# Loading one batch's q with four tokens per partition, transposing it for 512 tokens at once, and moving scores ahead of own values, in a fused retention and mixture-of-experts kernel

## The chip, the cores and the metric

The kernel runs on one core of one Trainium2 chip. The metric is the device time of one execution in microseconds (us); less is better. "Span" is the time from the first to the last instruction inside an execution, about 1.7 us less than the device time. Every run also reports the mean granted clock of TensorE as a share of full speed. All runs here are of the fast state; runs of one call share one chip and one set of runs of the kernel before. In the profile lines PE is TensorE, PEld its loading of weights, DVE VectorE, ACT ScalarE and POOL GpSimd. In this kernel the matmuls write to tiles in PSUM, everything else lies in SBUF; copying a PSUM tile to SBUF is called its eviction.

## The reference

```python
# q, k, v: (8 batches, 8 heads, 576 tokens, 64), fp32
scores = (1 / sqrt(64)) * q @ k.transpose          # per batch and head
gamma  = 1 - 2.0 ** (-5 - head)
Dmat   = where(i >= j, gamma ** (i - j), 0)        # causal decay
ret    = (scores * Dmat) @ v
x      = ret.transpose(0, 2, 1, 3).reshape(4608, 512)
p      = domain_probs / domain_probs.sum(-1)       # 4 experts
out    = sum_e p[:, e] * (relu(x @ w1[e]) @ w2[e]) # w1 512 x 1024, w2 1024 x 512
```

## The kernel before

The first part makes the retention output x of batch 0, 512 tokens in four "units" (two halves of the sequence by two groups of four heads) plus a "remainder" of 64 tokens. When x of the first 512 tokens is there, the dense expert matmuls start and go on to the end; later batches' retention is threaded into that stream in numbered slots. On TensorE: `pt` is a transpose, `s` the scores of a unit, `o` its values (own, from masked scores `sT`; carried, from the state `sbd`), `kvp` the products of k and v that make the state, `ph` and `po` the up and down matmuls of the experts, `or` the values of the remainder, `w` matmuls on zeros, put in to keep TensorE's clock up (with five more of them than the changed kernel has, 2 of 24 runs had a low mean clock, without them 16 of 24: f1 to f4, below).

```python
ring = ctx.enter_context(tc.tile_pool(name="ring", bufs=4, space=PSUM))   # every PSUM tile comes from here

def load_unit(raw, b, hf, g, eng):               # two tokens per partition: rows of 512 bytes
    for n, src in srcs:                          # k, q, v
        eng.dma_start(out=raw[n],
                      in_=src[b, 4 * g:4 * g + 4, 2 * C * hf:2 * C * hf + 2 * C, :]
                      .rearrange("h (p r) d -> p h (r d)", r=2))
# ... in values_carried: x is written from PSUM by ScalarE, back to natural token order
nat = lambda ap: ap.rearrange("p (a t r) -> p a r t", a=w, r=2)
src = lambda x, y: o[:, x:y, g, 0:C].rearrange("p a (r t) -> p a r t", r=2)
nc.scalar.activation(nat(xt_of(t)[:, p, lo:hi]), src(a, z), Copy)
# ...
load_w1_at = {1: (slice(0, F // 4),), 2: (slice(F // 4, F // 2), slice(F // 2, 3 * F // 4)),
              3: (slice(3 * F // 4, F),)}        # quarters of the first up weights, issued by GpSimd
# ...
for u in range(NU):
    if u + 2 < NU:
        cast_unit(u + 2)
    if u == NU - 1:
        part = UpHalf(0)
        part.matmuls(0)                          # 8 half-width up matmuls under the last mask
    us[u].values_own()
    if u == 2:
        us[3].kv(False, us[2].reads)
    if u + 1 < NU:
        us[u + 1].scores()
    if u == 1:
        us[2].kv(False, us[1].reads)
    us[u].values_carried()
    if u + 2 < NU:
        us[u + 2].trans_pe(1 - u)
    # ...
# ... slots of the dense stream: 19 scores of the remainder, 20 its values
for at, f in ((11, lambda: rem0.cast(nc.vector)), (11, rem0.trans_dma), (19, rem0.scores), (20, rem0.values)):
    add(at, f)
```

## Time and profile before

| | kernel before |
|---|---|
| device time, median of 6 runs of the same chip | 534.43 us (534.05 to 535.33) |
| span of the profiled run, granted clock | 532.9 us, 1.000 |
| start of the dense stream | 21.82 us |
| first values of the remainder (`or`) | 55.28 us |
| first kv products of batch 1 (`kvp`) | 59.85 us |

Four views matter besides those that the prediction shows. First, the stretch from 8 to 12 us in the view by windows (columns: window, length, busy us and number of instructions of PE, PEld, DVE, ACT and POOL, granted clock, DMA share, GB/s):

```profile
8.00:12.00 4.00, 3.34 (x58) 1.98 (x58) 3.68 (x6) 1.83 (x4) 1.46 (x2) 1.00 1.14 290
```

TensorE is busy 3.34 of 4 us and the clock is at 1.00. Second, ScalarE's copies of `o` into x, which close batch 0, in the groups of the first 30 us (columns: line, engine, operation, tiles, shapes, count, then busy us and mean ns, then the idle time before and what ended it): eight of 256 elements, 454 ns each.

```profile
L634 ACT ACTIVATE xt<-o 128x256 bf16<-128x256 f32 x8 | 3.1, 454 | 2.1 <-PE o L618 2.1
```

Third and fourth, the place where batch 1 enters the dense stream, in the timelines of TensorE and VectorE (columns: start, duration, engine, line, operation, tiles, shape, count, and in brackets the idle time before it and what ended it):

```profile
55.28 0.19 PE L333 MATMUL or<-sTr,bfr_v 128*128 128x64 bf16 x1 [0.37 <-DVE sTr L328]
...
59.51 0.42 PE L550 MATMUL s<-qkT 64*64 64x128 bf16 x16
59.85 0.72 PE L564 MATMUL kvp<-bf_v,bf_k 128*128 128x128 bf16 x8
60.51 0.40 PE L527 MATMUL pt<-ident,bf_k 128*128 128x128 bf16 x4
```

```profile
52.87 0.69 DVE L516 TENSOR_TENSOR bf_q<-raw_q,gq 128x512 bf16<-128x512 f32 x1 [0.21 <-DMA raw_q<-in_q_dram]
...
54.81 0.42 DVE L328 TENSOR_TENSOR sTr<-sr,trir 128x256 bf16<-128x256 f32 x1
...
58.85 1.40 DVE L399 SCALAR_TENSOR_TENSOR acc<-po,pm,acc 128x512 f32<-128x512 f32 x2
```

VectorE waits for the q rows of batch 1 (landed at 52.85), casts them, and only then makes `sTr` (ends 55.23) that `or` waits for at 55.28. So the start of `or` is already set by a transfer and by VectorE's queue behind it, 2.43 us after the rows land, not by TensorE's own work.

### The profile page before, as it was taken

Reading aid. Unit: us, or ns where it says so; the run is one execution under the profiler, and the core shown is the slowest. Engines: PE = TensorE matmul, PEld = TensorE weight load, DVE = VectorE, ACT = ScalarE, POOL = GpSimd, SP = SyncE. Lnnn points to the kernel's source line nnn. Section 1 sums busy time; section 2 is a strip of 40 time slices with the busy share of each in tenths; the row PEclk is TensorE's granted clock in tenths of the full one; section 3 lists DMA queues with packets and bytes.
Section 4 is the critical chain, followed back from the end, with each engine's and each line's share of the span. In section 5 each row is a group of like instructions: output and inputs, shape, how many; then the busy total and the mean of one; then the engine's idle time right before and its main releaser. Section 6 shows DMA issues by size and latency. Waiting matters only on the chain.

```text
span 532.9 us, 10183 instructions
## 1 busy us (share of the span) xinstructions
PE 523.0 (98%) x4212; PEld 341.4 (64%) x4251; DVE 363.1 (68%) x458; ACT 82.4 (15%) x167; POOL 151.8 (28%) x196
## 2 busy tenths in 40 slices
PE   7999999999999999999999999999999999999997
PEld 3644544478745885478646865587548844884486
DVE  5443968895577667697578767776765567557763
ACT  4722430012101111020101101110110000000010
POOL 5833404245244434235232604162000000000000
PEclk9999999999999999999999999999999999999999
DMA  9999977876769766737353664453010111110001
GB/s 238 181 214 219 244 192 183 171 159 163 153 164 158 169 141 149 162 77 173 95 136 92 149 134 115 104 129 116 20 41 25 56 39 41 41 41 20 1 22 59
DMA packets 146414, 63.74 MB, mean 120 GB/s; under 512 B 124608, under 2 KB 137168, under 8 KB 146368
## 3 DMA queue, kind: packets, MB, share of 16 engines
q1 hardware_dynamic: 134912, 43.61, 35.4%
q0 software_dynamic: 11312, 19.35, 16.9%
q8 instruction: 33, 0.54, 0.4%
q14 instruction: 13, 0.11, 0.1%
q10 hardware_dynamic: 144, 0.13, 0.1%
HBM read 53.56 MB, written 9.51 MB: 118 GB/s over the span
## 4 chain that ended last, share of the span: by engine, by line
PE 73%; ACT 2%; issue 0%; DVE 0%
PE ph L348 36%; PE pd L464 34%; ACT xt L291 2%; PE o L283 1%; PE o L278 1%; PE py L464 1%; DVE h L354 0%; PE or L333 0%; PE or L335 0%; PE sr L327 0%; DVE ob L492 0%
## 5 line engine op out<-in xcount | busy, mean ns | idle before, releaser
L348 PE MATMUL ph<-xt,w 128*128 128x512 bf16 x1103 | 248.6, 379 | 2.5 <-DVE h L354 0.2
L354 DVE SCALAR_TENSOR_TENSOR h<-ph,pB 128x1024 bf16<-128x1024 f32 x128 | 156.5, 1224 | 58.6 <-PE ph L348 57.8
L348 PEld LDWEIGHTS <-w 128*128 128x128 bf16 x1136 | 110.2, 98 | 128.5
L464 PEld LDWEIGHTS <-h 128*128 128x128 bf16 x1024 | 100.0, 98 | 13.3
L464 PEld LDWEIGHTS <-s 128*128 128x128 bf16 x768 | 75.0, 98 | 8.8
L464 PE MATMUL pd<-wx,h 128*128 128x256 bf16 x512 | 61.1, 273 | 0.2
L464 PE MATMUL pd<-wx,s 128*128 128x256 bf16 x512 | 61.1, 273 | 0.0
L219 POOL DMA_DIRECT2D pB<-pd x28 | 15.8, 564 | 154.7 <-DVE h L354 145.6
L499 POOL TENSOR_TENSOR ob<-v,p 128x256 f32<-128x256 f32 x15 | 11.8, 784 | 114.7 <-DVE v L496 86.6
L238 POOL TENSOR_TENSOR bf_k<-raw_k,gk 128x512 bf16<-128x512 f32 x24 | 26.1, 1088 | 36.0 <-DMA raw_k<-in_k_dram 16.3
L270 DVE TENSOR_TENSOR sT<-s,tri 128x1024 bf16<-128x1024 f32 x24 | 28.2, 1219 | 6.3 <-PE s L268 6.3
L437 DVE TENSOR_TENSOR s<-s,h 128x1024 bf16<-128x1024 bf16 x32 | 31.5, 1025 | 0.0
L291 ACT ACTIVATE xt<-o 128x768 bf16<-128x768 f32 (+6 forms) x24 | 13.0, 596 | 116.8 <-PE o L283 116.8
L464 PE MATMUL pd<-t4w,h 128*128 128x256 bf16 x256 | 30.6, 273 | 0.0
L387 PE MATMUL po<-wx,h 128*128 128x512 bf16 x123 | 28.7, 379 | 0.4 <-issue 0.2
L464 PE MATMUL pd<-t2w,s 128*128 128x256 bf16 x240 | 28.7, 273 | 0.0
L464 PE MATMUL pd<-t3w,h 128*128 128x256 bf16 x240 | 28.6, 273 | 0.0
L238 POOL TENSOR_TENSOR bf_q<-raw_q,gq 128x512 bf16<-128x512 f32 x24 | 27.0, 1125 | 4.2 <-DMA rawr_v<-in_v_dram 2.2
L472 ACT ACTIVATE p<-pd 128x256 f32<-128x256 f32 x16 | 6.2, 385 | 138.4 <-PE pd L464 106.2
L435 DVE TENSOR_TENSOR s<-h 128x1024 bf16<-128x1024 bf16 x32 | 24.3, 800 | 0.0
L441 DVE TENSOR_TENSOR s<-h,s 128x1024 bf16<-128x1024 bf16 x32 | 24.3, 800 | 0.0
L481 DVE TENSOR_TENSOR u<-pd,p 128x256 f32<-128x256 f32 x15 | 6.4, 425 | 22.3 <-PE pd L464 22.3
(155 smaller groups left out, 376.0 us busy)
## 6 DMA issues: line engine op xcount, KB each, us to landing
pB<-pd POOLq DMA_DIRECT2D x28, 256.0 KB, 3.6
raw_k<-in_k_dram SPq DMA_DIRECT2D x48, 128.0 KB, 2.9
raw_q<-in_q_dram SPq DMA_DIRECT2D x48, 128.0 KB, 3.0
raw_v<-in_v_dram SPq DMA_DIRECT2D x48, 128.0 KB, 3.1
out_dram<-oa SPq DMA_DIRECT2D x16, 256.0 KB, 2.2
out_dram<-ob SPq DMA_DIRECT2D x15, 256.0 KB, 2.2
w<-in_moe_w_dram POOLq DMA_DIRECT2D x3, 1024.0 KB, 13.5
wx<-in_moe_w_dram POOLq DMA_DIRECT2D x3, 1024.0 KB, 14.7
```

Source lines behind the costliest of these rows:

```text
L219: eng.dma_start(out=pB[t, e], in_=pd[e:e + 1, t * NT:(t + 1) * NT].to_broadcast([128, NT]))
L238: eng.tensor_tensor(bfs[p % 2][n], raw1[n], g[:, :, 2 * p:2 * p + 2].unsqueeze(3).to_broadcast([128, NC, 2, D]), op=MULT)
L270: nc.vector.tensor_tensor(sT[:, :, :, :].rearrange("p j c t -> p (j c) t"), s[:, :, :, :].rearrange("p j c t -> p (j c) t"), tri[:, :].uns ...
L291: nc.scalar.activation(xt_of(t)[:, self.ps, n0 + a - t * NT:n0 + z - t * NT], o[:, :, a:z], Copy)
L348: nc.tensor.matmul(ph[:, f, :], lhsT=w1_sb[e][:, dc, fc * 128:(fc + 1) * 128], rhs=x[:, dc, :], start=(dc == 0), stop=(dc == NDC - 1))
L354: nc.vector.scalar_tensor_tensor(h[:, fk:fk + 2, :], ph, 0.0, pB[t, e][:, :].unsqueeze(1).to_broadcast([128, 2, NT]), op0=MAX, op1=MULT)
L387: nc.tensor.matmul(po[:, gg, :], lhsT=h[:, e * NFC + fc, (2 * m + gg) * 128:(2 * m + gg + 1) * 128], rhs=wx[e // 2][:, (e % 2) * NFC + fc, ...
L435: nc.vector.tensor_tensor(self.alloc("s1")[:, l], h[:, l, self.b], h[:, r, self.b], op=ADD)
L437: nc.vector.tensor_tensor(self.alloc("s2")[:, l], self.s1[:, l], h[:, l, self.a], op=SUB)
L441: nc.vector.tensor_tensor(self.alloc("s4")[:, l], h[:, r, self.a], self.s2[:, l], op=SUB)
L464: mm = nc.tensor.matmul(dst, lhsT=src[:, kk, tok], rhs=rhs(c), start=(start and c == 0), stop=(c == KH - 1), skip_group_check=True)
L499: nc.gpsimd.tensor_tensor(self.ob[:, HF:Dm], self.v, self.p5, op=ADD)
```

## The change

The intent: read q of batch 0 in longer rows (four tokens, 1,024 bytes), transpose it for the whole sequence at once, and give VectorE the scores of the next unit before TensorE does the own values of the present one. With it come a different split of the weight loads, another place for the up matmuls, and one slot for the remainder.

```diff
+                nc.sync.dma_start(out=flat(raw0q[u][:, 2 * gg:2 * gg + 2, :, :]),
+                                  in_=q[0, 4 * u + 2 * gg:4 * u + 2 * gg + 2, 0:SM, :]
+                                  .rearrange("h (p r) d -> p h (r d)", r=4))
 ...
-                    nat = lambda ap: ap.rearrange("p (a t r) -> p a r t", a=w, r=2)
-                    src = lambda x, y: o[:, x:y, g, 0:C].rearrange("p a (r t) -> p a r t", r=2)
+                    rr = 2 if self.b else 4
+                    nat = lambda ap: ap.rearrange("p (a t r) -> p a r t", a=w, r=rr)
+                    src = lambda x, y: o[:, x:y, g, 0:C].rearrange("p a (r t) -> p a r t", r=rr)
 ...
+    load_w1_at = {1: quarter[0:1], 2: quarter[1:2], 3: quarter[2:4]}
 ...
     for u in range(NU):
         if u + 2 < NU:
             cast_unit(u + 2)
-        if u == NU - 1:
-            part = UpHalf(0)
-            part.matmuls(0)
-        us[u].values_own()
-        if u == 2:
-            us[3].kv(False, us[2].reads)
         if u + 1 < NU:
             us[u + 1].scores()
-        if u == 1:
-            us[2].kv(False, us[1].reads)
+        if u + 2 < NU:
+            us[u + 2].trans_pe()
+        if u == 3:
+            warm(2)
+        us[u].values_own()
+        if u in (1, 2):
+            us[u + 1].kv(False, us[u].reads)
         us[u].values_carried()
 ...
-    part.matmuls(1)
+    part = [UpHalf(i) for i in range(2)]
+    for i in range(2):
+        part[0].matmuls(i)
+        part[1].matmuls(i)
 ...
-    ... (19, rem0.scores), (20, rem0.values)):
+    ... (19, rem0.scores), (21, rem0.values)):
```

Cut are the tables for four tokens, the casts and transposes of q by themselves, the number of matmuls on zeros (19 before, 16 after), the move of two state copies from VectorE to ScalarE, and the relus of the two up halves, which now both follow the 32 up matmuls.

More of the change, by code (lines that the diff above doesn't have):

```diff
@@ L112 @@
     NU = 4
-    raw0 = [{n: epool.tile([128, 4, 2, D], FP32, name=f"raw0_{u}{n}") for n, _ in srcs} for u in range(NU)]
-    bf0 = {n: spool.tile([128, 2, 2, 2, 4, D], BF16, tag="S", name=f"bf0_{n}") for n, _ in srcs}
+    raw0 = [{n: epool.tile([128, 4, 2, D], FP32, name=f"raw0_{u}{n}") for n in "kv"} for u in range(NU)]
+    raw0q = [epool.tile([128, 4, 4, D], FP32, name=f"raw0_q{g}") for g in range(2)]
+    bf0 = {n: spool.tile([128, 2, 2, 2, 4, D], BF16, tag="S", name=f"bf0_{n}") for n in "kv"}
+    bf0q = spool.tile([128, 2, 4, 4, D], BF16, tag="S", name="bf0_q")
+    q4 = [epool.tile([128, 2, 4, C], BF16, name=f"q4_{g}") for g in range(2)]
     def load_unit(raw, b, hf, g, eng):
         for n, src in srcs:
-            eng.dma_start(out=raw[n],
-                          in_=src[b, 4 * g:4 * g + 4, 2 * C * hf:2 * C * hf + 2 * C, :]
-                          .rearrange("h (p r) d -> p h (r d)", r=2))
+            if n in raw:
+                eng.dma_start(out=raw[n],
+                              in_=src[b, 4 * g:4 * g + 4, 2 * C * hf:2 * C * hf + 2 * C, :]
+                              .rearrange("h (p r) d -> p h (r d)", r=2))
     units0 = ((0, 0), (0, 1), (1, 0), (1, 1))
@@ L125 @@
     for u, (hf, g) in enumerate(units0):
-        load_unit({n: raw0[u][n][:, :, :, :].rearrange("p h r d -> p h (r d)") for n in "kqv"}, 0, hf, g, nc.sync)
+        flat = lambda t: t.rearrange("p h r d -> p h (r d)")
+        load_unit({"k": flat(raw0[u]["k"][:, :, :, :])}, 0, hf, g, nc.sync)
+        if u < 2:
+            for gg in range(2):
+                nc.sync.dma_start(out=flat(raw0q[u][:, 2 * gg:2 * gg + 2, :, :]),
+                                  in_=q[0, 4 * u + 2 * gg:4 * u + 2 * gg + 2, 0:SM, :]
+                                  .rearrange("h (p r) d -> p h (r d)", r=4))
+        load_unit({"v": flat(raw0[u]["v"][:, :, :, :])}, 0, hf, g, nc.sync)
     zz = epool.tile([128, 512], BF16)
@@ L143, with pair_mask @@
     make_identity(nc, ident)
-    tri0 = tpool.tile([128, 2, 2, C // 2], BF16, tag="uv", name="tri0")
-    nc.gpsimd.memset(tri0, 1.0)
-    for a in range(2):
-        nc.gpsimd.affine_select(out=tri0[64 * a:64 * a + 64], in_=tri0[64 * a:64 * a + 64],
-                                compare_op=mybir.AluOpType.is_ge, fill=0.0,
-                                base=0, channel_multiplier=-2, pattern=[[-1, 2], [1, 2], [2, C // 2]])
+    pos_4 = epool.tile([128, 4], FP32)
+    nc.gpsimd.iota(pos_4, pattern=[[1, 4]], base=0, channel_multiplier=4, allow_small_or_imprecise_dtypes=True)
+    def pair_mask(t, r):
+        nc.gpsimd.memset(t, 1.0)
+        for a in range(2):
+            nc.gpsimd.affine_select(out=t[64 * a:64 * a + 64], in_=t[64 * a:64 * a + 64],
+                                    compare_op=mybir.AluOpType.is_ge, fill=0.0,
+                                    base=0, channel_multiplier=-2, pattern=[[-1, 2], [1, r], [r, C // r]])
+    tri4 = epool.tile([128, 2, 4, C // 4], BF16, name="tri4")
+    pair_mask(tri4, 4)
+    tri0 = tpool.tile([128, 2, 2, C // 2], BF16, tag="uv", name="tri0")
     nc.gpsimd.memset(sbd, 0.0)
@@ L160 @@
     decays(gk0, gq0, (lambda o, h: o[:, :, h, :], pos_0))
+    gq4 = const.tile([128, H, 4], FP32, name="gq4")
+    for hh in range(H):
+        nc.vector.tensor_scalar_mul(gq4[:, hh, :], pos_4, -lg[hh])
+    nc.scalar.activation(gq4, gq4, Exp, scale=-1.0, bias=lsc)
     tri = const.tile([128, C], BF16)
@@ L171, in later_tables @@
     def later_tables():
+        pair_mask(tri0, 2)
         nc.gpsimd.memset(tri, 1.0)
@@ L517, in cast, with trans_pe @@
                                  .unsqueeze(3).to_broadcast([128, 4, 2, D]), op=MULT)
-        def trans_pe(self, between=0):
+        def trans_pe(self):
             self.qk = atp.tile([128, 2, 2, 2, C], BF16, tag="qkT", name="qkT0")
             pt = ring_tile("pt", [128, 2, 2, 2, 2 * C], BF16)
-            for i, n in ((1, "k"), (0, "q")):
-                if i == 0 and between:
-                    warm(between)
+            ns = ((1, "k"), (0, "q")) if self.b else ((1, "k"),)
+            for i, n in ns:
                 for r in range(2):
@@ L528, in trans_pe @@
                                             self.bf(n)[:, r, 2 * g:2 * g + 2].rearrange("p j d -> p (j d)"), ident)
-            nc.scalar.activation(self.qk[:, :, :, :, :].rearrange("p i r g t -> p i (r g) t"),
-                                 pt[:, :, :, :, 0:C].rearrange("p i r g t -> p i (r g) t"), Copy)
+            lo = 2 - len(ns)
+            nc.scalar.activation(self.qk[:, lo:2].rearrange("p i r g t -> p i (r g) t"),
+                                 pt[:, lo:2, :, :, 0:C].rearrange("p i r g t -> p i (r g) t"), Copy)
         def trans_dma(self):
@@ L538, in qT @@
         def qT(self, rows, g, a):
+            if self.b == 0:
+                i = 64 * self.hf + 32 * a
+                return q4[self.g][rows, g, :, i:i + 32]
             return self.qk[rows, 0, :, g, 64 * a:64 * a + 64]
@@ L554, in scores @@
                 s[:, :, :, :, :].rearrange("p j g r t -> p (j g) (r t)"),
-                tri0[:, :, :, :].rearrange("p r s t -> p (r s t)").unsqueeze(1).to_broadcast([128, 4, 2 * C]), op=MULT)
+                (tri0 if self.b else tri4)[:, :, :, :].rearrange("p r s t -> p (r s t)").unsqueeze(1).to_broadcast([128, 4, 2 * C]), op=MULT)
         def kv_mm(self, rows, dst, hh, start=False, others=()):
@@ L592, in kv @@
                 else:
-                    self.reads.append(nc.vector.tensor_copy(dst, src) if not fresh and self.g == 0 else nc.scalar.activation(dst, src, Copy))
+                    self.reads.append(nc.scalar.activation(dst, src, Copy))
                 if hf == 0 and self.carry is not None:
@@ L641, in values_carried, with cast_q, trans_q @@
                     a = z
-    bfv0 = lambda g: {(n, hf): bf0[n][:, hf, g] for n in "kqv" for hf in range(2)}
+    bfv0 = lambda g: {(n, hf): bf0[n][:, hf, g] for n in "kv" for hf in range(2)}
     us = [Unit(0, hf, g, raw0[u], bfv0(g)) for u, (hf, g) in enumerate(units0)]
-    warm(8)
-    us[0].cast("k", nc.vector)
-    us[0].cast("q", nc.vector)
-    us[0].cast("v", nc.gpsimd)
-    us[0].trans_pe()
-    warm(3)
-    load_w1_at = {1: (slice(0, F // 4),), 2: (slice(F // 4, F // 2), slice(F // 2, 3 * F // 4)),
-                  3: (slice(3 * F // 4, F),)}
+    def cast_q(g):
+        for gg in range(2):
+            hs = slice(2 * gg, 2 * gg + 2)
+            nc.vector.tensor_tensor(
+                bf0q[:, g, :, hs, :].rearrange("p r h d -> p h r d"), raw0q[g][:, hs, :, :],
+                gq4[:, 4 * g + 2 * gg:4 * g + 2 * gg + 2, :].unsqueeze(3).to_broadcast([128, 2, 4, D]), op=MULT)
+    def trans_q(g):
+        pt = ring_tile("ptq", [128, 2, 4, C], BF16)
+        for gg in range(2):
+            for r in range(4):
+                nc.tensor.transpose(pt[:, gg, r, :], bf0q[:, g, r, 2 * gg:2 * gg + 2, :].rearrange("p j d -> p (j d)"),
+                                    ident)
+        nc.scalar.activation(q4[g], pt, Copy)
+    quarter = [slice(i * F // 4, (i + 1) * F // 4) for i in range(4)]
+    load_w1_at = {1: quarter[0:1], 2: quarter[1:2], 3: quarter[2:4]}
     def cast_unit(u):
         us[u].cast("k", nc.vector)
-        us[u].cast("q", nc.vector)
+        if u < 2:
+            cast_q(u)
         us[u].cast("v", nc.gpsimd)
@@ L658, in cast_unit @@
             load_w1(0, f)
+    warm(8)
+    cast_unit(0)
+    us[0].trans_pe()
+    warm(2)
+    trans_q(0)
+    warm(4)
     cast_unit(1)
+    us[1].trans_pe()
     us[0].scores()
-    warm(4)
-    us[1].trans_pe(2)
+    trans_q(1)
     us[0].kv()
-    warm(1)
     for u in range(NU):
@@ L668 @@
             cast_unit(u + 2)
-        if u == NU - 1:
-            part = UpHalf(0)
-            part.matmuls(0)
-        us[u].values_own()
-        if u == 2:
-            us[3].kv(False, us[2].reads)
         if u + 1 < NU:
             us[u + 1].scores()
-        if u == 1:
-            us[2].kv(False, us[1].reads)
+        if u + 2 < NU:
+            us[u + 2].trans_pe()
+        if u == 3:
+            warm(2)
+        us[u].values_own()
+        if u in (1, 2):
+            us[u + 1].kv(False, us[u].reads)
         us[u].values_carried()
-        if u + 2 < NU:
-            us[u + 2].trans_pe(1 - u)
         if u == 0:
@@ L692 @@
     h = hp.tile([128, E * NFC, NT], BF16, name="h")
-    part.relu(h)
-    part = UpHalf(1)
-    part.matmuls(0)
-    part.matmuls(1)
-    part.relu(h)
+    part[0].relu(h)
+    part[1].relu(h)
     first = ctx.enter_context(ExitStack())
@@ L745 @@
     rem0 = Rem(0)
-    for at, f in ((11, lambda: rem0.cast(nc.vector)), (11, rem0.trans_dma), (19, rem0.scores), (20, rem0.values)):
+    for at, f in ((11, lambda: rem0.cast(nc.vector)), (11, rem0.trans_dma), (19, rem0.scores), (21, rem0.values)):
         add(at, f)
```

## The prediction

> **What bounds the kernel now.** I read the page's busy shares first, then the chain that ended last, then the waits of TensorE, then the timeline of the first 25 us, because the diff touches only batch 0 and one slot later on.
>
> ```profile
> PE 523.0 (98%) x4212; PEld 341.4 (64%) x4251; DVE 363.1 (68%) x458; ACT 82.4 (15%) x167; POOL 151.8 (28%) x196
> PE 73%; ACT 2%; issue 0%; DVE 0%
> ...
> PE s L550 <- ACT qkT L529: 0.5, 1, 0.5
> PE pt L527 <- DVE bf_k L516: 0.4, 1, 0.4
> PE or L333 <- DVE sTr L328: 0.4, 1, 0.4
> ```
>
> TensorE is busy for 523 of 532.9 us and carries the chain; its named waits are a few tenths each. The busy share flatters the start, though: warm-up matmuls on zeros (`w`) count as work, and so does pipeline time. What matters is when the dense stream of 512-column matmuls begins, since after it the order and number of matmuls are the same in both kernels, apart from one slot. In the timeline:
>
> ```profile
> 16.87 0.42 PE L550 MATMUL s<-qkT 64*64 64x128 bf16 x16
> 17.34 1.23 DVE L552 TENSOR_TENSOR sT<-s,tri 128x1024 bf16<-128x1024 f32 x1 [0.88 <-PE s L550]
> 17.45 1.04 PE L369 MATMUL ph<-xt,w 128*128 128x256 bf16 x8
> 18.62 0.42 PE L608 MATMUL o<-sT,bf_v 64*64 64x128 bf16 x16
> 18.97 0.40 PE L618 MATMUL o<-qkT,sbd 128*128 128x128 bf16 x4
> 19.20 2.78 PE L369 MATMUL ph<-xt,w 128*128 128x256 bf16 x24
> ```
>
> This is the end of batch 0. While VectorE masks the last unit's scores (17.34 to 18.57), TensorE does 8 of the 32 half-width up matmuls; own values, carried values and the other 24 follow. 24 matmuls at 0.109 us (8 took 0.87 us from first start to ninth) put the start of the dense stream at 19.20 + 2.62 = **21.82 us**.
>
> What feeds the start is the queue of loads. Each line gives KB and the time from issue to landing:
>
> ```profile
> raw_0k<-in_k_dram SPq DMA_DIRECT2D x1, 256.0 KB, 2.8
> raw_0q<-in_q_dram SPq DMA_DIRECT2D x1, 256.0 KB, 3.1
> raw_0v<-in_v_dram SPq DMA_DIRECT2D x1, 256.0 KB, 4.9
> raw_1k<-in_k_dram SPq DMA_DIRECT2D x1, 256.0 KB, 5.3
> raw_1q<-in_q_dram SPq DMA_DIRECT2D x1, 256.0 KB, 5.6
> ```
>
> With their issue times in the timeline (0.81, 1.33, 1.87, 2.41, 2.96) they land at 3.6, 4.5, 6.8, 7.7 and 8.6: one 256 KB load per 0.90 us (about 290 GB/s), with one stall of 1.4 us before the third.
>
> [...] zero matmuls go from 0.427 to 0.216 us apart at 5.5 us [...] with a granted clock of 1.00.
>
> **The change part by part.**
>
> *Loads.* The same 3 MB in 12 loads, but q of both halves of the sequence comes with the first two units. Order before: k q v, four times. After: k0 q q v0, k1 q q v1, k2 v2, k3 v3. The piece that completes unit 1's q moves from fifth to seventh place. Landings, with the stall in third place as now: k0 3.6, q 4.4, q 6.65, v0 7.55, k1 8.45, q 9.25, **q 10.05**, v1 10.95, k2 11.85, v2 12.7, k3 13.6, v3 14.4. The last comes 0.3 us earlier (4 x 0.10), the first two units 1.5 to 2.2 us later.
>
> *Work.* Transposes of q: 16 before and after. Casts of q: 4 at 0.69 before and after. Copies of transposed data on ScalarE: 4 x 1.025 before; after, 4 of half size at an estimated 0.59 (between the rows of 256 elements at 0.38 to 0.45 and 1,024 at 1.025) and 2 x 1.025, so 4.4 against 4.1 us. Two copies of carried state (2 x 0.42 us) go from VectorE to ScalarE. Zero matmuls: 19 before, 16 after. VectorE gets 8 small multiplies of some 0.1 us before the first load lands, which is free. Nothing large is removed: this is a change of order.
>
> *The path after.* Following the new order of instructions with these durations and about 0.05 us for each handover:
> 1. q lands at 10.05; VectorE casts it: 10.1 to 10.8.
> 2. Four transposes, drained: 11.25. ScalarE copies (1.02): 12.3.
> 3. Scores of unit 1 (0.42): 12.35 to 12.9. Mask (1.22): to 14.2.
> 4. VectorE, in order, casts k of unit 3 only now, though it landed at 13.6: 14.1 to 14.8; transposes from 15.05, copied (0.59) by 16.1.
> 5. TensorE meanwhile: own values of unit 1 (0.25), kv of unit 2 (0.65 with its two switches), carried values (0.11), front of kv for unit 3 (0.44), with switches of tile shape at about 0.09: scores of unit 3 start at 17.0.
> 6. Mask of unit 3: 17.5 to 18.7. Under it lie own values of unit 2, kv of unit 3, carried values of unit 2 and the two new zero matmuls, to 18.85.
> 7. Own and carried values of unit 3: 18.95 to 19.5.
> 8. Then all 32 half-width matmuls, 32 x 0.109 = 3.5: the dense stream starts at **23.0**.
>
> The same reckoning on the order of before gives 22.05 where the trace has 21.82, so I use differences: 23.0 - 22.05 = **+0.95 us**. Of that, 0.87 is step 8: the 8 up matmuls that filled the wait for the last mask now stand behind it, with zero matmuls in their old place. Putting scores ahead of own values does shorten each unit, but the later q of unit 1 eats it.
>
> *Remainder.* Values of the first remainder move one slot (8 matmuls of 0.216 = 1.7 us) later, behind which their wait of **0.37** (listed above) vanishes.
>
> Sum: 534.35 + 0.95 - 0.37 = 534.9 us.
>
> **The rivals.**
> - *The stall before the third load does not come back.* Nothing in the profile says what makes it, and fewer, longer rows may avoid it. Then q of unit 1 lands at 9.0, and the same steps start the dense stream at 21.97, or 0.08 less than before: 534.35 - 0.08 - 0.37 = 533.9 us. I give this one in three.
> - *The weights become the bound.* The second half of the first w2 is issued at 16.75 and lands at 26.8; its first matmul is at 25.27 + 8 x 0.216 = 27.0, a slack of 0.2. Had the change made TensorE earlier by 1 us, the weights would have taken most of it back. With TensorE later, and the load queue relieved by 0.3 us, they do not bind. The same slack caps any gain.
> - *ScalarE becomes the bound of batch 0.* It gets the q copies and both state copies, and the two final copies of o (0.77 a pair) now come in one run of four after the last state copy. The up matmuls of the second half need them at 20.4, they end at about 20.5, and only their fourth quarter is needed last. Close, 0 to 0.3 us.
> - *The clock falls back.* Idle stretches of some 1.3 us (waiting for the second q piece) and 0.7 us are larger than before's[...]. Chance 5%, cost 1 to 2 us.
>
> **Range and chances.** Two thirds of 534.9 and one third of 533.9 give 534.6. The runs of before spread over 1.3 us and the load times are uncertain by about 0.5 us, so 533.5 to 535.7 should hold 8 times in 10. Two per cent is 10.7 us, and the whole of batch 0 takes 22: within 2% is as good as certain.
>
> **What would show it.** In the profile of the changed kernel: the second q piece of unit 1 lands near 10 (9 if the stall is gone); the last carried values at about 19.3 and then 32 half-width matmuls in one run of 3.5 us; the first 512-column matmul near 22.8; no wait of `or` on `sTr`; loads of w2 landing by 27 with no wait on them. The prediction is wrong if q in 1,024-byte rows lands much faster than 0.8 us a piece, if TensorE waits for weights, or if the zero matmuls run at 0.427 us again after 6 us.

The 0.80 us for a 256 KB piece of q in 1,024-byte rows was the author's assumption: the kernel before has no such rows, and its 256 KB loads land 0.90 us apart but for one stall. The 5% for the clock rests on the assumption that idle stretches of 1.3 and 0.7 us leave it alone, which was not shown either. The small terms of the path are in the trace of the kernel before: from the end of a cast on VectorE to the first transpose 0.06 us (5.18 to 5.24), a switch of tile shape 0.10 us (16 matmuls of own values take 0.25 us up to the next start at 10.78, where the same shape follows, and 0.35 at 18.62, where another does), seven small multiplies on VectorE 0.71 us (1.20 to 1.91).

## The result, and the profile after

The changed kernel took **538.37 us** (median of 6 runs, 536.19 to 540.25) against 534.43. A ratio is the mean time of one kernel's fast runs over the mean of the other's of the same rounds, so not quite the ratio of the medians: 1.0072, with a 95% interval of 1.0043 to 1.0102. So it is within 2%, as predicted, but 2.7 us above the top of the range. The spread tripled, too: 4.1 us between runs, against 1.3, and four of the six runs had a mean clock of 0.990 to 0.997. The profile fell on a run of 540.11 us (span 538.4, clock 0.997).

The end of batch 0, in TensorE's timeline, then in ScalarE's groups of the first 30 us, then in ScalarE's timeline:

```profile
19.14 0.40 PE L645 MATMUL o<-q,sbd 128*128 128x128 bf16 x4
19.37 1.67 PE L393 MATMUL ph<-xt,w 128*128 128x256 bf16 x11
21.34 2.45 PE L393 MATMUL ph<-xt,w 128*128 128x256 bf16 x21 [0.30 <-ACT xt L662]
23.84 1.46 PE L372 MATMUL ph<-xt,w 128*128 128x512 bf16 x6
```

```profile
L662 ACT ACTIVATE xt<-o 128x256 bf16<-128x256 f32 x8 | 5.1, 799 | 0.0
```

```profile
18.84 2.45 ACT L662 ACTIVATE xt<-o 128x256 bf16<-128x256 f32 x4
```

The last carried values start at 19.14, where the prediction had 19.3. But the 32 half-width matmuls (11 and 21) are held up twice by the run of four copies on ScalarE, which took 2.45 us; each copy took 799 ns where the kernel before had 454. The last half-width matmul starts at 23.52, so the dense stream begins at 23.63 (the record of its first matmul is missing, the one shown is the second). That is 1.81 us later than before; 0.95 was predicted.

Batch 1's entry, in the timelines of TensorE and VectorE:

```profile
58.28 0.19 PE L357 MATMUL or<-sTr,bfr_v 128*128 128x64 bf16 x1
...
60.78 0.42 PE L577 MATMUL s<-qkT 64*64 64x128 bf16 x16
63.35 0.72 PE L591 MATMUL kvp<-bf_v,bf_k 128*128 128x128 bf16 x8 [2.15 <-DVE acc L423]
...
65.11 2.92 PE L411 MATMUL po<-wx,h 128*128 128x512 bf16 x7 [0.22 <-issue]
```

```profile
55.45 0.69 DVE L540 TENSOR_TENSOR bf_q<-raw_q,gq 128x512 bf16<-128x512 f32 x1 [0.21 <-DMA raw_q<-in_q_dram]
...
57.39 0.42 DVE L352 TENSOR_TENSOR sTr<-sr,trir 128x256 bf16<-128x256 f32 x1
...
61.90 1.40 DVE L423 SCALAR_TENSOR_TENSOR acc<-po,pm,acc 128x512 f32<-128x512 f32 x2
```

The wait of `or` is gone, as predicted. In its place the kv products stand still for 2.15 us until VectorE has done `acc`, the eviction of a `po` tile, at 63.29. They need its PSUM buffer: with one slot later, the ring of four buffers hands the kv products another buffer than before, and in the program's semaphores they wait for `acc` where they had waited for a transpose on TensorE. VectorE is late because the q rows landed at 55.43 instead of 52.85. After the standstill seven `po` matmuls start 0.427 us apart instead of 0.216 (2.92 us for 7): the clock has fallen, to 0.50 from 64.21 to 67.62.

The whole difference of the two profiled spans, 5.5 us, adds up from these lines: dense stream 23.63 - 21.82 = +1.81; the wait of `or` that is gone, -0.54 (in the kernel before, `s` of batch 1 comes 37.69 us after the dense start; after, 37.15); the wait of the kv products, +2.22 (63.35 instead of 60.78 + 0.35); slow clock until own values, +1.68 (4.61 us from kv products to own values at 67.96 instead of 2.93); everything later, +0.33.

### The profile page after: what moved, and what is told of

Read it like the earlier page. It is cut to its first block, busy times and chain, and to the rows that moved or that the text cites. A ratio compares the mean times of both kernels' runs of the same rounds, so it can differ in the third digit from the quotient of the medians.

```text
span 538.4 us, 10193 instructions
## 1 busy us (share of the span) xinstructions
PE 525.3 (98%) x4209; PEld 342.2 (64%) x4248; DVE 363.9 (68%) x464; ACT 85.4 (16%) x172; POOL 153.3 (28%) x200
## 4 chain that ended last, share of the span: by engine, by line
PE 72%; ACT 2%; issue 0%; DVE 0%
PE ph L372 36%; PE pd L488 33%; ACT xt L315 2%; PE o L307 1%; PE o L302 1%; PE py L488 1%; DVE h L378 0%; PE or L357 0%; PE sr L351 0%; PE or L359 0%; DVE ob L516 0%
## 5 line engine op out<-in xcount | busy, mean ns | idle before, releaser
L488 PEld LDWEIGHTS <-h 128*128 128x128 bf16 x1024 | 100.0, 98 | 13.3
L411 PEld LDWEIGHTS <-h 128*128 128x128 bf16 x128 | 12.5, 101 | 15.0 <-issue 1.6
```

The costliest lines, as they stand in the source:

```text
L411: nc.tensor.matmul(po[:, gg, :], lhsT=h[:, e * NFC + fc, (2 * m + gg) * 128:(2 * m + gg + 1) * 128], rhs=wx[e // 2][:, (e % 2) * NFC + fc, ...
L488: mm = nc.tensor.matmul(dst, lhsT=src[:, kk, tok], rhs=rhs(c), start=(start and c == 0), stop=(c == KH - 1), skip_group_check=True)
```

## The experiments

Eighteen further kernels ran, all correct. In the table, "low clock" counts runs with a mean clock of 0.998 or less.

| run | what it is | median us (range) | ratio to before, 95% | low clock |
|---|---|---|---|---|
| changed kernel | | 538.37 (536.19 to 540.25) | 1.0072, 1.0043 to 1.0102 | 4 of 6 |
| e1 | slot 20 back | 537.62 (536.18 to 538.02) | 1.0055, 1.0040 to 1.0070 | 4 of 6 |
| e2 | eviction turned | 537.17 (536.00 to 540.25) | 1.0061, 1.0035 to 1.0087 | 4 of 6 |
| e3 | e1 and e2 | 536.88 (535.36 to 538.09) | 1.0040, 1.0023 to 1.0057 | 4 of 6 |
| e4 | before with slot 21 | 534.28 (533.90 to 535.25) | 0.9999, 0.9986 to 1.0012 | 0 of 6 |
| f1 | changed, 5 zero matmuls more | 537.03 (536.49 to 540.82) | 1.0062, 1.0035 to 1.0088 | 1 of 6 |
| f2 | e3, 5 zero matmuls more | 536.86 (535.36 to 537.67) | 1.0042, 1.0024 to 1.0059 | 1 of 6 |
| f3 | f2, early up matmuls | 536.14 (535.09 to 537.30) | 1.0031, 1.0014 to 1.0048 | 0 of 6 |
| f4 | f2, old order | 536.56 (535.46 to 537.70) | 1.0039, 1.0021 to 1.0056 | 0 of 6 |
| g1 | f3, weights' quarter back | 535.57 (534.98 to 536.48) | 1.0015, 1.0001 to 1.0028 | 0 of 5 |
| g2 | changed, quarter back | 537.59 (535.91 to 538.61) | 1.0049, 1.0030 to 1.0068 | 3 of 6 |
| g3 | before, quarter late | 535.40 (534.76 to 536.70) | 1.0010, 0.9995 to 1.0026 | 0 of 6 |
| g4 | g1, slot 21 | 536.18 (534.98 to 537.19) | 1.0024, 1.0008 to 1.0040 | 2 of 6 |
| h1 | changed, VectorE's order | 539.32 (535.91 to 541.48) | 1.0078, 1.0046 to 1.0110 | 4 of 6 |
| h2 | g1, VectorE's order | 535.38 (534.49 to 536.15) | 1.0015, 0.9999 to 1.0031 | 1 of 6 |
| h3 | before, VectorE's order | 534.09 (533.70 to 536.51) | 1.0001, 0.9981 to 1.0021 | 0 of 6 |
| h4 | f1, slot 20, VectorE's order | 536.84 (536.61 to 538.15) | 1.0046, 1.0031 to 1.0061 | 1 of 6 |
| i1 | f1, the wait lengthened | 538.98 (538.42 to 540.01) | 1.0090, 1.0072 to 1.0107 | 1 of 4 |
| i2 | i1, slot 20 | 540.01 (538.70 to 540.55) | 1.0099, 1.0082 to 1.0117 | 3 of 4 |

In the 51 runs of the kernel before beside these, the mean clock was never under 0.999.

### The slot and the eviction, each alone and together (e1, e2, e3), and the slot in the kernel before (e4)

```diff
 e1, e3:  -(21, rem0.values)
          +(20, rem0.values)
 e2, e3:  -nat = lambda ap: ap.rearrange("p (a t r) -> p a r t", a=w, r=rr)
          +nat = lambda ap: ap.rearrange("p (a t r) -> p a r t" if self.b else "p (a t r) -> p a t r", a=w, r=rr)
          -src = ... .rearrange("p a (r t) -> p a r t", r=rr)
          +src = ... .rearrange("p a (r t) -> p a r t" if self.b else "p a (r t) -> p a t r", r=rr)
 e4:      kernel before, -(20, rem0.values)  +(21, rem0.values)
```

> The changed kernel with one part undone: the values of a unit's remainder stand in the earlier slot again (20 instead of 21). Theory A (buffer rotation): in the changed kernel the first kv products of batch 1 take the buffer that the eviction of po on VectorE frees late (a wait of 2.15 us at 63.35, after which the matmuls ran at 0.43 us instead of 0.21 for about 2.5 us). With the slot back, that wait and the slow matmuls vanish, and a wait of about 0.4 us before those values comes back: about 536.0 us, 2.3 under the changed kernel. Theory B (late transfers): the batch 1 rows land 2.5 us later whatever the slot is, and TensorE waits elsewhere for the same lateness: 537.5 to 538.5 us. Either way the run's first part (dense stream from about 23.6) is as in the changed kernel.

> The changed kernel with the eviction of o to xt on ScalarE turned round in batch 0: it writes neighbouring tokens (2-byte step) and reads PSUM with the step instead; the result stays right. Theory A (the step of the writes costs): an eviction of 128x256 takes 0.35 to 0.45 us instead of 0.80, the last ones end about 0.7 to 1.0 us earlier, the first 512-column matmul stands at about 22.7 instead of 23.6, and the time falls by about 0.9 us if the later wait on the kv products stays as it is (537.4). Theory B (any strided 128x256 eviction costs this): 0.75 to 0.85 us each, no change, 538.3.

> Both edits of the two runs before: values of the remainder back in the earlier slot, and the eviction of batch 0 writing neighbouring tokens. If both theories A hold and add up: 535.1 us, within 0.5 of the kernel before. If neither: 538.3.

> The kernel before with only the values of the remainder moved one slot later (21 instead of 20). Theory A (rotation): the same new dependency of the kv products on the eviction of po, but rows land 2.5 us earlier here and VectorE's eviction ended at 60.25 when the products were due at about 59.85: a wait of 0.4 us in place of the 0.37 us that is taken away: 534.1 to 535.0 us. If the wait is long enough for the clock to fall, 536 to 537. Rival (the slot is a plain gain of 0.37): 534.0.

**The eviction** is settled in the profile; the time of e2 (537.17, 537.4 expected) lies too near that of the changed kernel to show 0.9 us. Turned round, it writes neighbouring tokens and takes its step in PSUM instead; the copies fall from 799 to 381 ns, in ScalarE's groups of the first 30 us of e2:

```profile
L662 ACT ACTIVATE xt<-o 128x256 bf16<-128x256 f32 x8 | 2.6, 381 | 0.3 <-PE o L645 0.2
```

So it is the 8-byte step of the writes that costs, not the four tokens as such: the kernel before writes with a step of 4 bytes at 454 ns.

**The slot** did what theory A said in the profile: with slot 20 (e1, e3) the kv products follow the scores after 0.35 us, with slot 21 (e2) after 1.07, and there they start 0.06 us after `acc` ends, as in the changed kernel. But the times missed: 536.0 was expected of e1 and 537.62 came, which lies in the range of theory B, though no wait stands at batch 1 in e1's profile; of e3 535.1 was expected and 536.88 came. Alone in the kernel before (e4) the slot changes nothing (ratio 0.9999): the wait of `or` went, and the kv products waited 0.05 us more.

Why e1 missed shows in the view by windows of its own profile:

```profile
8.00:12.00 4.00, 2.55 (x51) 1.72 (x52) 3.69 (x5) 2.31 (x5) 1.45 (x2) 0.98 1.20 301
12.00:15.50 3.50, 3.50 (x49) 2.19 (x39) 1.82 (x2) 2.63 (x6) 3.00 (x5) 0.53 1.05 158
```

The granted clock is 0.53 from 12 to 15.5 us, the same in e2 (0.54) and e3 (0.60). The profile of the changed kernel has the same thin stretch, without the fall:

```profile
8.00:12.00 4.00, 2.54 (x42) 1.50 (x41) 3.66 (x5) 2.32 (x4) 1.41 (x2) 1.00 1.21 300
```

In both, TensorE is busy 2.54 to 2.55 of the 4 us from 8 to 12, instead of 3.34 (3.73 in e4), because the new order waits there for the pieces of q, for their casts and for ScalarE's copy, and has fewer matmuls on zeros to fill those waits. This was a new theory (C): too thin a stretch lets the clock fall, in some runs and not in others.

### Holding the clock, and the other parts of the start (f1 to f4)

```diff
 f1 to f4:  -    warm(4)                       +    warm(6)
            +            if self.b == 0 and (self.hf, self.g) == units0[1]:      # in scores()
            +                for _ in range(3):                                     # zeros, overwritten after
            +                    nc.tensor.matmul(s[:, 0].rearrange("p g r t -> p (g r t)"),
            +                                     lhsT=zz[:, 0:128], rhs=zz, start=True, stop=True)
 f2, f3, f4: and the edits of e3
 f3:        -            warm(2)
            +            part = [UpHalf(0)]
            +            part[0].matmuls(0)
 f4:        the loop's order of the kernel before: own values, kv, scores, carried values, transposes
```

> The changed kernel plus five matmuls on zeros in its two emptiest places in batch 0: two more before the k transposes of unit 1, three before its scores (written to the scores' own buffer and overwritten). Three earlier profiles of variants showed the granted clock at 0.5 for 3 to 3.5 us from 12 on, after a stretch of 8.3 to 11.7 in which matmuls streamed only about 0.38 of the time (0.56 or more in the kernel before). Theory C (too thin a stretch lowers the clock at the start in most runs): no matmul at half speed between 6 and 20, mean clock 1.0 in every run that hasn't the long wait at 61 to 63; runs of 537 to 538 become 536.0 to 536.4, the runs at 539 to 540 (wait of the kv products) stay possible. Theory D (the fall is random or from elsewhere): runs at 0.996 to 0.997 as often as in the changed kernel, median 537 to 538.

> The same five zero matmuls, with the values of the remainder back in the earlier slot and the eviction writing neighbouring tokens. Theory C with both theories A: the slow runs vanish altogether, every run has clock 0.999 to 1.0, median 535.4 (that of the two runs of the pair without zeros whose clock was 1.0), spread about 1 us. Theory D: median 536.9 as without the zeros.

> As the run before, and eight half-width up matmuls instead of two matmuls on zeros under the last mask, where the kernel before has them. Prediction's step 8: 8 x 0.109 = 0.87 us leave the end of batch 0, the two zero matmuls (0.43) beside the mask lengthen nothing: 0.5 to 0.9 us less, 534.5 to 534.9. Rival (the up matmuls wait for the eviction of o or for weights there): 535.4, and a wait of the first of them.

> As the second run of this call, with the old order within a unit: own values first, then the scores of the next unit, transposes last. It measures what the order alone is worth, given the new q. If the scores ahead of own values shorten each unit, as the prediction held without a figure: 0.3 to 1.0 us slower than with the new order (535.7 to 536.4). If VectorE's masks and casts decide the pace of the units whatever TensorE's order is: the same within 0.2 us (535.4).

The clock held: none of the four profiles shows a fall after 6.5 us, and 2 of 24 runs had a low mean clock, against 16 of 24 of the changed kernel, e1, e2 and e3. Over everything that ran (without i1 and i2), 23 of 36 runs with the change's zero matmuls have a low clock and 6 of 47 with five more. The 23 average 538.55 us, the other 13 of the 36 average 536.29, so a run with a low clock is 2.3 us longer on average. That the thin stretch lets the clock fall is supported by this; what it should bring to the median is not, as follows.

The traces, cut up afterwards, say which stretches let it fall. In the eight falls of the kept profiles before 520 us the clock stays low for 3.41 us, and each fall comes a whole number of such stretches after the clock's first rise (in the changed kernel's profile it rises at 6.18 and falls at 64.21, 17 of them later). Take the columns of the matmuls that start in each of these stretches, at 0.216 us for 512, and weigh them by the size of their tile as a part of 128*128, the largest in the traces (a quarter for 64*64). In all 20 profiles the eight stretches that end in a fall are filled to between 0.21 and 0.38, and every other one at full clock to 0.41 or more. The plain busy share does not part them: 0.32 to 0.65 before a fall, and down to 0.55 without one. The thinnest stretch in the start of the changed kernel's profile has 0.41, those of e1 to e3 have 0.36 to 0.38: the start lies just at the edge, so where the cuts fall would decide from run to run. This was found after the fact; no run was made to test it.

The pieces of the start can be read from the profiles as the time from the landing of the last q piece to the dense stream:

| run | q complete | dense stream | between | what differs |
|---|---|---|---|---|
| changed | 9.63 | 23.63 | 14.0 | |
| f1 | 9.69 | 23.81 | 14.1 | zeros |
| f2 | 9.64 | 22.84 | 13.2 | and the eviction turned: -0.9 |
| g1 | 9.57 | 22.35 | 12.8 | and up matmuls early: -0.4 |
| f4 | 10.09 | 24.19 | 14.1 | f2 with the old order: +0.9 |
| e3 | 9.63 | 24.11 | 14.5 | f2 without zeros, clock fell: +1.3 |
| e1 | 9.41 | 24.81 | 15.4 | f1 without zeros, clock fell: +1.3 |

f2 in TensorE's timeline has all 32 half-width matmuls in one run and the dense stream at 22.84:

```profile
19.35 3.66 PE L393 MATMUL ph<-xt,w 128*128 128x256 bf16 x32
22.84 2.32 PE L372 MATMUL ph<-xt,w 128*128 128x512 bf16 x10
...
56.59 0.19 PE L357 MATMUL or<-sTr,bfr_v 128*128 128x64 bf16 x1 [0.66 <-DVE sTr L352]
```

But the medians hardly moved (f1 537.03 where 536.2 was expected, f2 536.86 where 535.4 was). The last of these lines shows where the gain went: `or` now waits 0.66 us for `sTr`, which ended 2.38 us after the q rows of batch 1 landed at 54.16. In each of the four profiles with slot 20 that have this wait and VectorE's old order (before, f2, g1, g3) the values of the remainder start 2.43 us after those rows; in each of the five with slot 21 in which the kv products wait for `acc` (changed, e2, e4, f1, g4) these start 7.5 to 7.9 us after them. An earlier start of the dense stream is given back there when the rows are late. In f1 TensorE also loses 0.56 us at 174 us to a transfer of remainder rows, which the profile of the kernel before does not show.

f3 landed at 536.14, 1.2 us over its expected range. Its eight early up matmuls do run under the last mask, but 0.58 us of the gain was lost because the second half's matmuls stood ahead of the first half's rest and waited for ScalarE; g1 mends that. f4 lost 0.9 us at the start by the old order, so **scores ahead of own values gain 0.9 us at the start**. That is one profile each, but the measure repeats well: f1, h4, i1 and i2, whose starts are equal, have 14.12 to 14.13 us. The median of f4 (536.56) is not above f2's: the gain at the start does not show in the time.

### Why the rows are late (g1 to g4)

```diff
 g1, g2, g4:  -load_w1_at = {1: quarter[0:1], 2: quarter[1:2], 3: quarter[2:4]}
              +load_w1_at = {1: quarter[0:1], 2: quarter[1:3], 3: quarter[3:4]}
 g3:          kernel before, the third quarter moved from unit 2 to unit 3
 g1, g4:      built on f3, the first half's up matmuls finished first; g4 with (21, rem0.values)
```

> The kernel with five zero matmuls, turned eviction, earlier slot and early up matmuls, and now also the third quarter of the first up weights issued with unit 2, as the kernel before has it, and the first half's up matmuls finished before the second half's begin. Theory E (the quarter that the change issues 1.3 us later leaves the software queue idle, and everything behind it in that queue, up to the rows of batch 1, lands about 1.2 us later, where VectorE's casts and then TensorE wait for them): w2 of the third expert pair lands at 51 to 51.5 instead of 51.5 to 53.8, the q rows of batch 1 at 52.9 or so, dense stream from about 22.2, time 534.2 to 534.8, spread 1.5 us. Rival (the lateness comes from elsewhere, from chip to chip or run to run): landings as in the profile without this edit (53.2), 535.5 to 536.2.

> The changed kernel with that quarter alone issued with unit 2 again. Theory E: rows of batch 1 land 1.2 us earlier, the wait of the kv products at 61 to 63 shrinks to under 1 us in nearly every run, so no runs at 539 to 540.8, while the start stays as it was: 536 to 537.8, median 537.0. Rival: runs at 539 and more as often as in the changed kernel (3 of 6).

> The kernel before with that quarter alone issued with unit 3, as the change does. Theory E: the software queue idles about 1.2 us, rows of batch 1 land about 1.2 us later, and the wait of the remainder's values, 0.37 us, grows by as much: 535.4 to 535.8 us. Rival (the queue catches up, or the rows weren't what that wait came from): 534.3 to 534.7.

> The first kernel of this call with the values of the remainder in the change's slot. With the rows on time, the wait of about 0.4 us for the remainder goes and the wait of the kv products stays under 0.3: 533.9 to 534.5, the best of all, level with the kernel before or up to 0.5 better. If the rows are late in some runs, those show 536 to 538.

Theory E is not confirmed as the main cause. Only g3 came as it expected (535.40); g1 (535.57) lies in the rival's range, g2 (537.59, 537.0 expected) had three runs of 538.5 to 538.6, and g4 (536.18) took 1.7 us more than expected. With the quarter late, the q rows of batch 1 landed at 55.43 (changed kernel) and at 53.16 to 54.16 (e1 to e3, f1 to f4); with it restored at 53.09, 54.63 and 54.04, no clear difference. With the start of the kernel before they landed at 52.85 (before) and 51.70 (e4). With the quarter late there (g3) they landed at 53.52, `or` lost 0.87 us instead of 0.54, and TensorE lost 0.50 us at 27.33 to the second half of the first down weights, which landed at 27.29 instead of 26.77 (the prediction gave that load a slack of 0.2). g3's ratio of 1.0010 is some 0.5 us, with an interval that still holds 1. So the quarter may do some harm, of a few tenths. A single load between them, half of the third expert pair's down weights, landed 6.2 to 7.7 us after the load before it, from profile to profile, so part of the lateness is a matter of the run. What makes the rest, 1 us or so, was not tested. The traces narrow it down: the second half of the first down weights already lands at 27.73 on average in the changed kernel, e1 to e3 and f1 to f4, against 26.07 in before, e4 and h3, so the lateness is there before 28 us. GpSimd issues the first quarter of the up weights after its cast of v of unit 1, which lands at 10.53 in the changed kernel instead of 9.47; that issue moves from 10.08 to 11.14.

The start of g4 shows another weak point of the new order of loads: the second piece of q landed at 7.08 instead of 6.1, TensorE had nothing to do until then, and its granted clock was 0.57 on average from 8 to 12 us in spite of the zeros. The profile of h2, below, has the same (second piece at 6.86, clock low from 7.57 to 10.98).

### VectorE's queue behind the rows (h1 to h4)

```diff
 +    for which in (3, 1):
 +        add(18, lambda which=which: w_sum(which, 0, 4))   # t3w and wx, ahead of the casts of batch 1
 # and, not shown here, both are left out of the loop that added them to slot 18 before
 h1: changed kernel; h2: g1; h3: kernel before; h4: f1 with (20, rem0.values)
```

> The changed kernel with one exchange in VectorE's queue: the two weight differences (t3w and wx, 0.69 us each) stand ahead of the two casts of batch 1's first rows instead of behind them, so they run while VectorE would only wait for those rows. Theory F (late rows, then what VectorE has queued behind them, set when the kv products start: the products start 0.06 us after the second eviction acc, and that ends 7.4 to 7.9 us after the q rows land, in every run with slot 21): acc ends about 6.9 us after the q rows land instead of 7.8, the wait shrinks by 0.7 to 1.0 us, the runs at 539 to 540.8 come down to 536.5 to 538.5; median 536.8 to 537.4. Rival (the wait comes from somewhere else, such as GpSimd's cast of v): unchanged, 538.0 to 538.6.

> The best version so far (five zero matmuls, turned eviction, slot 20, early up matmuls, the weights' quarter early) with the same exchange in VectorE's queue. In its last profile the remainder's values waited 0.25 us for sTr, which ended 2.4 us after the q rows of batch 1 landed. Theory F: sTr comes about 1 us sooner after the rows, the wait goes and runs with late rows are no longer longer: 534.6 to 535.2, spread 1.2 us. Rival (only the start of the dense stream counts): 535.6 as before the exchange.

> The kernel before with the same exchange alone. Its values of the remainder waited 0.37 us for sTr in the profile, plus 0.17 beside it. Theory F: this wait is set by the rows as well and goes: 0.2 to 0.5 us faster, 534.0 to 534.3. Rival: no change within 0.15 us.

> The changed kernel with zero matmuls in its two gaps, slot 20, and the exchange in VectorE's queue, so that the clock holds and neither late wait is left, while the eviction with the 8-byte step, the late up matmuls and the late quarter of weights stay. What is left over the kernel before should be the later dense stream alone, 23.8 instead of 21.8 (0.9 for the eviction, 0.9 for the up matmuls), less the 0.5 of waits that the kernel before has: 1.5 us, so 536.0 to 536.4, spread 1.5. If it stays at 537 the sum misses something.

In the profiles theory F holds: in h1 `acc` ends 6.3 us after the rows instead of 7.9 and the kv products follow the scores at once; in h3 `sTr` ends 1.16 us after the rows instead of 2.38 and `or` waits for nothing; nor does it in h2 and h4. In the times it does not show: h3 has a ratio of 1.0001, h2 of 1.0015 as g1 (535.38, just over the range of theory F), and h1 took 539.32, a miss by 2. Its profile fell on a run of 535.91 us; four of its six runs took 538.7 to 541.5 with a mean clock of 0.986 to 0.994. A mean of 0.986 means about 15 us at a clock of 0.50 (an estimate: 0.014 of 538 us, over 0.50), four stretches of 3.41 us, the length and the clock seen in e1. Where these lie no profile has shown, and shortening VectorE's queue does not prevent them. h4 came to 536.84, 0.4 over the upper end expected of the sum.

### The wait lengthened on purpose (i1, i2)

```diff
 -            add(at, lambda which=which, j=j: w_sum(which, 4 * j, 4 * j + 4))
 +            for _ in range(3 if j == 0 and which == 3 else 1):
 +                add(at, lambda which=which, j=j: w_sum(which, 4 * j, 4 * j + 4))
 both on f1; i2 with (20, rem0.values)
```

> The changed kernel with five zero matmuls at the start (clock held there), and the suspected wait made longer on purpose: VectorE computes the first weight difference three times instead of once behind the late rows (2 x 0.69 = 1.4 us more before the evictions that the kv products of batch 1 wait for). Theory A with F: the kv products wait about 1.4 us longer than without (0.2 to 2.2 us there), 2 us or more in most runs; in those the clock falls after it, for one stretch of 3.4 us or more: 538.5 to 541.5, mean clock 0.99 to 0.997 in most runs, and a profile that shows where. Rival (the wait is long only where the transfers are slow, and what lowers the clock is something else in the same runs): 537.8 to 538.6, clock 1.0.

> The same with the values of the remainder in the earlier slot: the same work stands in VectorE's queue, but what waits is the remainder's values, for sTr. If the slot matters only through the total of waits, this is as slow as the run beside it. Theory A with F: sTr ends 3.8 us after the q rows land instead of 2.4, the values wait 0.3 to 1.5 us more, no idle stretch is long enough for the clock to fall: 537.3 to 538.3, clock 0.999 to 1.0, 1 to 3 us faster than the run beside it.

With 1.4 us more in VectorE's queue, i1 took 1.95 us more than f1 (medians; other chips, on which the kernel before differs by 0.4). The intervals of the two ratios overlap, but the profiles show the wait: the kv products stand still for 1.76 us in i1 and 0.02 in f1. i2 took 3.2 us more than h4, but h4 also has both weight differences ahead of the rows, so four pieces of 0.69 us lie between them, 2.8 us and not 1.4. So the rows and what VectorE does behind them do set the pace here. But both expectations failed in part: i1 had a low clock in one run of four and not in most, and i2, with the earlier slot, is not faster (540.01 against 538.98). TensorE's timeline of i1, then of i2:

```profile
63.16 0.72 PE L595 MATMUL kvp<-bf_v,bf_k 128*128 128x128 bf16 x8 [1.76 <-DVE acc L423]
```

```profile
59.44 0.21 PE L357 MATMUL or<-sTr,bfr_v 128*128 128x64 bf16 x1 [2.80 <-DVE sTr L352]
...
59.84 3.14 PE L411 MATMUL po<-wx,h 128*128 128x512 bf16 x8
```

In i2 the standstill of 2.80 us is followed by eight matmuls in 3.14 us, where the next eight, at 63.27, take 1.89; in i1, after one of 1.76 us, eight take 1.89. So the clock can fall after a long standstill with slot 20 too, as it did with slot 21 after 2.15 us in the changed kernel, and what the slot decides is which wait is exposed and by how much. At the delays of the changed kernel slot 21 is the worse one: 13 of the 36 runs with it took over 538.4 us (changed kernel, e2, f1, g2, g4, h1), none of the 47 with slot 20 and the new q (i1 and i2 left out). Without the five zero matmuls it is 12 of 24 against 0 of 12, with them 1 of 12 against 0 of 35, so the zeros seem to matter as much as the slot. With a longer delay slot 20 has no such advantage: all eight runs of i1 and i2 took over 538.4.

No version with the new q beat the kernel before. The best, h2, is at 535.38 us against 534.44 in its rounds; the interval of its ratio, 0.9999 to 1.0031, just holds 1.

## Why the prediction was right or wrong

Steps 1 to 7 held; three terms failed: the length of step 8, the wait of the remainder that was taken away with nothing put in its place, and the 5% for the clock.

- **Loads: right.** The q pieces landed 0.78 to 0.80 us apart (0.80 assumed; the 512-byte rows of the kernel before take 0.90), the stall came back in third place, though shorter (4.62 to 6.32, 0.9 us beyond a piece instead of 1.4), and q was complete at 9.63, 0.4 us before the 10.05 expected.
- **Steps 1 to 7: right.** The last carried values came at 19.14 (19.3 expected), when the clock held.
- **Step 8: the term was mis-sized.** The prediction took 32 x 0.109 = 3.5 us; it lasted 4.26 (19.37 to 23.63). The failed assumption is in the rival on ScalarE, "the two final copies of o (0.77 a pair)", taken over from a kernel that writes with another step. A pair in a run of four cost 1.23; the rival's "0 to 0.3 us" should have been 0.8 to 0.9. With the eviction turned round (f2) the 32 matmuls took 3.49 and the dense stream started at 22.84, where the prediction had 22.8. That it fits so well is partly luck: q came 0.4 us earlier than predicted, and the way from there took 0.45 longer. The 0.87 for the up matmuls was too large as well: with 8 of them back under the last mask (g1) the dense stream came 0.4 us sooner, because there they outlast the mask (it ends at 18.42, own values start at 19.14).
- **Remainder: half right.** The 0.37 us (0.54 with what stood beside it) went. That a buffer ring hands out its buffers in another order, so that the kv products now wait for `acc`, was not considered at all: 2.2 us in the profiled run, 0.1 to 0.7 in e2, f1 and g4.
- **"The load queue relieved by 0.3 us": wrong.** The row loads did end 0.66 us earlier (14.01; the prediction's own "4 x 0.10" is 0.4), but the weights behind them came later (the second half of the first w2 at 28.01, not by 27, though without a wait), and the rows of batch 1 landed 2.6 us later in the profile; in e1 to e3 and f1 to f4 they landed at 53.79 on average, 1.55 later than in the three profiles with the start and weights of the kernel before (before, e4, h3: 52.25). I read the waits of TensorE alone, and not that its wait of `or` on `sTr` was itself a wait for a transfer.
- **The clock: the fall was named, its chance was wrong.** The rival gave 5% and 1 to 2 us. It happened in 4 of 6 runs of the changed kernel and in 23 of 36 with its zero matmuls, at 1.3 us a fall in the start and 1.7 in the profiled run at batch 1. The 5% rested on the author's assumption that idle stretches of 1.3 and 0.7 us do no harm, and that was the step that failed. The clock fell after a gap of 2.15 us at batch 1, and at the start of e1 to e3 after gaps of 0.4 to 0.6 us each in the stretch before the fall, of which the matmuls, weighed by tile, filled 0.36 to 0.38.
- **Range: too narrow** because it took its spread from the kernel before, whose clock stayed at 0.999 or more in all 51 runs. The class, within 2%, was right.

The sum of what is shown: later start 1.8 (0.9 from the order of the up matmuls, 0.4 by g1, and the later q together, 0.9 from the eviction), less 0.5 of waits, plus 0 to 5 us of slow clock and of waits for batch 1 that vary from run to run; runs in which the clock held lie at 536.3 on average, those in which it fell at 538.55. That 13 of 36 runs with slot 21 are over 538.4 and none of 47 with slot 20 is a count, not a mechanism: the part of it that h1's slow runs make stays open.

## What to carry to other kernels

Keep matmuls on zeros, or better useful ones, wherever TensorE waits in the start of a kernel (five more on zeros: a low clock in 2 of 24 runs instead of 16 of 24), and judge a stretch by how much of it its matmuls fill, weighed by tile, not by its longest gap: in the traces here every stretch of 3.41 us at full clock that was filled to 0.38 or less ended in a fall and none filled to 0.41 or more did, while the clock fell in e1 to e3 with gaps of 0.4 to 0.6 us and held in i1 after one of 1.76. When four tokens share a partition, let the step of un-interleaving fall on the PSUM read and not on the SBUF write (381 ns a copy in e2, 799 in the changed kernel). Before gaining time ahead of a wait, ask what that wait itself depends on: here a transfer of later rows set the pace at 55 us, so a gain at 20 us was returned and a delay was not; and when a user of a buffer ring moves, look at who waits for whose buffer afterwards.
